# A new issue order for every step of a two-stage kernel (RWKV-7 recurrence, then SwiGLU), with its tiles, operations and bytes kept

## The chip, the cores and the metric

The kernel runs on one NeuronCore of one Trainium2 chip. The metric is device microseconds of one execution, as the median of three runs. Engines are named as the profile does: PE is TensorE's matmuls and PEld its weight loads, DVE is VectorE, ACT is ScalarE, POOL is GpSimd, SP is SyncE. SP and POOL issue nearly all DMAs here, each in the order in which they stand in its own queue.

## What is computed

Everything is float32. The first part is a recurrence over 768 tokens for 4 x 8 heads with a 40 x 40 state; the second part is a gated feed-forward layer over the 3072 tokens of width 320.

```python
for t in range(S):                       # S = 768, per batch and head
    y[:, :, t] = einsum('bhd,bhde->bhe', rt, state)
    Sa = einsum('bhde,bhe->bhd', state, at)
    state = state * wt[:, :, None, :] - einsum('bhd,bhe->bhde', Sa, bt)
    state = state + einsum('bhd,bhe->bhde', vt, kt)
x = y.transpose(0, 2, 1, 3).reshape(3072, 320)
xn = x / sqrt(mean(x * x, -1) + 1e-6) * rms_g
g = xn @ w_gate                          # 320 x 1536
out = (g * sigmoid(g) * (xn @ w_val)) @ w_out
```

## The kernel before

The tokens are worked in 24 chunks of 32, and all 32 heads of a chunk together. Five kinds of stages are written one after another in program text.

- `narrow(k)`, 24 of them: the weights arrive as 64-bit floats, are turned into 32-bit ones with ACT and DVE, and are written back to DRAM as twelve slices `sW0` to `sW11` of 480 KB each.
- `front(c)` for chunk c: loads w and a (tile `wan`), k and b (tile `kbn`), w again (`wn`) and v (`VU`), transposes them on PE, and builds products level by level (matmuls into `ps` from `A`, `Ab` and `K`; results into `KN` and `LT`). It ends by passing a triangular matrix through DRAM (`sB` from `LT`, then `M` from `sB`).
- `inverse(c)`: a chain of 62 dependent DVE operations (`tmp` from `Yi` and `M`, then `Yi` minus `tmp`), through DRAM again (`sY` from `Yi`, `LT` from `sY`). The first four chunks use a shorter form with small matmuls (`M`).
- `main(c)`: the recurrence from chunk to chunk: matmuls from `ST` and `aP` (called state below), from `VU` and `LT` (lower), from `Xs` (lower), from `VU` and `KN` (update), then DVE writes the next `ST`; beside it the scores (`rE`, `vut`), the levels (`As` with `KN` or `kbn`), the output `y`, its norm and its transposition into `xg`.
- `feed(g)` for two chunks together, 12 of them: for each pair of weight slices the loads `wf` from `sW`, matmuls `ps` from `xg` and `wf`, a SiLU on ACT (`sg`), a product on DVE (`hT`), and matmuls `po` from `wf` and `hT`; at the end `o` goes to `out_dram`. Six `wf` buffers hold three pairs, so a load has to wait until the matmuls that read its buffer before are done.

In program text this order isn't issued. Each step becomes a piece of a plan with its engine and its dependences, and `Plan.issue` then issues all 5870 pieces in the order of a table, `ORDER`. A number in it is the distance of the next piece from the first piece that isn't issued yet; a `-` is a filler: one 128 x 128 matmul of the identity into an unused strip of `po` (two matmul records each in the profile, since float32 matmuls take two passes). A second table, `PAIRS`, gives each PSUM result (`room`) one of three bank pairs, `ps0` to `ps2`. Each engine works its own pieces strictly in the issued order, so the tables decide which piece stands ahead of which on each engine and queue; semaphores do the rest.

```python
plan.warm = lambda: nc.tensor.matmul(po_[:, 0, DM:DM + P], ident, ident, start=False, stop=False, skip_group_check=True)
with tc.manual_schedule():
    plan.issue(ORDER, PAIRS)
```

Nearly all instructions of a kind share one line, that of the helper which records them: L503 for DVE, L523, L526 and L529 for ACT, L532 to L538 for POOL, L542 for all DMAs, L545 for matmuls, L548 for transposes, L1077 for the fillers. The profile is therefore read by tiles.

Of the kernel before, what the change touches and what calls it, by code (L numbers as in the profile page):

```python
# [33 lines left out]
- - 4 - 327 - 328 - - - 6 453 5 7 8 9 10 - 11 12 13 14 15 - 16 17 19 18 20 25 26 21 316 325 - - 313 314 324  # L34
323 - 326 318 - 315 317 93 74 83 3 94 85 73 84 82 - 320 46 43 50 61 38 - - - 60 - - 445 444 455 49 58 44 27 56
62 - 333 41 36 48 54 70 - 441 66 53 59 45 638 29 - 32 28 456 55 451 - - - 442 - 334 339 - - 337 335 338 340
349 350 23 - 342 343 354 24 353 22 355 348 351 352 - 344 - 362 336 366 364 95 - 345 367 346 - - - 347 379 360
- - - 361 363 - 359 365 - 375 75 76 376 78 - 79 - 387 77 356 357 - - 373 - 86 378 371 377 - 80 452 446 454 443
57 - 525 636 37 458 34 368 461 - 374 372 89 386 - 369 383 358 462 - 384 370 466 464 465 385 463 478 98 483 495
- 380 467 381 87 468 395 477 - - 470 471 482 - - 481 472 96 492 382 88 494 97 - 99 - 491 476 493 0 328 123 - -  # L40
102 0 - 100 320 - - 121 112 390 389 387 388 102 - - 111 123 392 471 477 487 - 478 486 - 472 98 - - 488 391 79
103 485 473 88 - - - 89 505 626 61 631 69 598 524 633 621 31 67 66 37 395 632 - - 482 - 62 623 622 28 635 625
- 33 396 624 29 397 398 399 483 400 - - 498 401 402 403 404 405 406 407 - - - - - - - 494 499 484 504 - - 394
500 511 502 496 - 104 - 408 409 410 501 411 412 413 414 - 386 - 415 - 503 416 417 418 419 420 421 422 - 641
105 646 - 106 645 643 - 642 - 107 - 423 - 424 425 - 108 497 - 510 - 644 495 426 328 99 330 329 577 427 - - 506
508 509 109 317 319 120 - 90 - 124 647 521 513 - 125 648 113 114 - 115 657 - 522 131 132 576 - 339 507 127 650
651 656 128 - 428 110 142 517 516 - 652 143 518 515 429 - 653 658 512 660 661 - 116 - 654 - 659 117 655 567
860 70 38 - 45 457 65 63 445 446 448 870 861 871 458 447 430 50 - 662 126 568 669 - 133 134 135 578 581 580
579 672 674 - 664 - - - 118 - - - 519 - 520 - - - 431 - - 432 434 433 - 435 - 436 670 437 438 569 572 570 573
571 129 663 673 675 136 137 138 525 683 - 526 527 671 684 467 528 665 529 667 679 668 682 530 531 532 687 680  # L50
686 533 534 535 536 537 538 539 540 685 541 676 677 542 514 543 544 545 546 547 548 549 550 551 552 553 554 -
119 151 140 162 160 - 163 802 141 999 152 666 582 - 574 144 678 681 583 688 147 148 689 555 1000 172 0 761 90
131 535 653 105 516 546 - - 551 - 555 - 564 - 99 659 121 657 658 660 549 550 553 554 552 654 113 650 106 - 114
109 547 655 548 115 116 117 589 590 600 118 0 406 656 590 600 508 548 554 547 825 579 657 700 701 816 509 131
101 643 115 550 551 552 118 642 119 647 702 703 116 117 124 1083 125 126 652 134 653 511 110 512 143 513 510
553 556 557 558 658 559 560 - 120 561 654 831 514 132 826 835 834 515 832 133 135 833 127 128 129 659 660 661
662 663 664 665 666 667 138 142 - 121 516 517 136 137 836 704 706 655 144 708 705 707 - 139 840 - 668 669 670
671 841 - 852 672 848 140 851 853 673 147 674 - 675 148 - 676 865 677 863 861 0 683 - 689 700 694 685 690 684
459 868 693 707 581 708 717 732 734 582 15 579 716 548 712 580 549 713 550 714 719 715 432 585 23 - - 33 21 0
- 394 11 33 32 13 0 26 25 16 861 683 - 417 418 862 681 419 851 749 750 671 571 0 708 701 569 0 569 - 5 6 416  # L60
531 572 689 532 8 533 534 9 708 535 386 704 566 14 15 16 17 - - 0 - 570 569 568 699 529 530 698 567 0 528 700
0 562 713 711 14 698 715 15 559 7 8 712 560 567 710 406 855 16 - 724 427 854 844 21 417 22 568 569 570 571 575
709 716 667 708 - 528 574 573 - 0 23 22 33 520 - 696 782 563 698 784 785 783 697 705 711 567 568 708 709 569
570 571 - 710 398 399 400 401 713 - 847 836 841 830 840 832 842 831 572 769 - - 839 - 829 521 21 0 16 - - 516
712 24 515 710 709 517 711 514 - 841 843 844 842 565 704 840 6 566 848 0 0 0 760 846 856 853 857 564 565 566
712 567 - 569 570 568 - 759 761 842 713 573 - 515 575 574 843 4 852 14 15 16 703 6 844 7 851 17 847 516 5 0
509 568 1243 703 702 846 850 858 0 9 509 858 14 15 16 860 568 569 570 753 523 21 24 23 1241 22 707 708 846 10
709 839 840 710 859 856 754 755 756 757 841 861 711 712 713 850 853 854 714 715 869 716 - 717 718 866 871 872
852 - 855 0 560 561 32 755 513 756 - 857 840 851 854 852 708 862 709 710 711 712 713 714 853 856 - 759 863 864
# [1040 lines left out]
```

## Time and profile before

| What | Value |
|---|---|
| runs, median | 1030.82 us |
| runs, lowest and highest of 3 | 1029.99 and 1036.54 us |
| the profiled execution, its own time | 1040.74 us |
| the profiled execution, its span | 1038.9 us |
| mean granted TensorE clock in it | 0.970 |
| busy in the span: PE, DVE, ACT, POOL | 991.8, 834.2, 452.8, 310.1 us |

The profiled execution took 9.92 us more than the median of the runs and 4.2 us more than the slowest of them, and its span is 1.84 us shorter than its time. Numbers of the trace are those of this one execution; "busy" is time in which an engine had at least one instruction running, and the clock is the share of full speed that PE was granted. "issue" as a releaser means that the engine waited for nothing that the profile shows.

### The profile page before, as it was taken

Reading aid. Unit: us, or ns where it says so; the run is one execution under the profiler, and the core shown is the slowest. Engines: PE = TensorE matmul, PEld = TensorE weight load, DVE = VectorE, ACT = ScalarE, POOL = GpSimd, SP = SyncE. Lnnn points to the kernel's source line nnn. Section 1 sums busy time; section 2 is a strip of 40 time slices with the busy share of each in tenths; the row PEclk is TensorE's granted clock in tenths of the full one; section 3 lists DMA queues with packets and bytes.
Section 4 is the critical chain, followed back from the end, with each engine's and each line's share of the span. In section 5 each row is a group of like instructions: output and inputs, shape, how many; then the busy total and the mean of one; then the engine's idle time right before and its main releaser. Section 6 shows DMA issues by size and latency. Waiting matters only on the chain.

```text
span 1038.9 us, 56159 instructions
## 1 busy us (share of the span) xinstructions
PE 991.8 (95%) x24900; PEld 813.4 (78%) x24900; DVE 834.2 (80%) x2789; ACT 452.8 (44%) x1019; POOL 310.1 (30%) x554
## 2 busy tenths in 40 slices
PE   8968798999999999999999999999999999999998
PEld 7867686888887888888778877878777788787876
DVE  8878777887979898899888798888899789889310
ACT  5755783644452543433533443352334334341210
POOL 9624422231451224142134232242331331210000
PEclk9886898999999999999999999999999999999999
DMA  7676567465443434534433644343524533422322
GB/s 156 155 171 162 156 130 187 127 160 135 124 87 93 120 73 94 131 72 92 127 71 81 139 79 126 94 84 83 140 61 93 136 67 83 130 44 63 87 65 75
DMA packets 163538, 113.03 MB, mean 109 GB/s; under 512 B 124512, under 2 KB 142880, under 8 KB 163296
## 3 DMA queue, kind: packets, MB, share of 16 engines
q1 hardware_dynamic: 144928, 86.48, 32.9%
q0 software_dynamic: 16192, 22.64, 10.9%
q8 instruction: 195, 3.19, 1.3%
q10 hardware_dynamic: 2176, 0.33, 0.3%
q14 instruction: 47, 0.39, 0.1%
HBM read 93.39 MB, written 15.99 MB: 105 GB/s over the span
## 4 chain that ended last, share of the span: by engine, by line
PE 77%; DVE 10%; DMA 4%; issue 4%; ACT 3%; POOL 1%; SPq 1%; ACTq 0%; DVEq 0%; POOLq 0%
PE ps L545 51%; PE po L545 13%; PE ps L548 7%; PE po L1077 5%; DVE LT L503 2%; DVE tmp L503 2%; DVE Yi L503 2%; DVE K L503 1%; DMA kbn<-in_k_dram 1%; SPq L542 1%; DMA wf<-sW 1%; ACT K L526 1%; DVE As L503 1%; ACT KN L526 1%; DMA kbn<-in_b_dram 1%
## 5 line engine op out<-in xcount | busy, mean ns | idle before, releaser
L545 PE MATMUL ps<-xg,wf 128*128 128x256 f32 (+1 forms) x1728 | 356.8, 394 | 1.6 <-DVE ST L503 0.5
L545 PEld LDWEIGHTS ps<-xg,wf 128*128 128x128 f32 (+1 forms) x1728 | 264.7, 191 | 51.1 <-issue 14.0
L545 PE MATMUL po<-wf,hT 128*128 128x320 f32 x576 | 173.6, 440 | 1.7 <-issue 1.1
L523 ACT ACTIVATE sg<-ps 128x512 f32<-128x512 f32 x72 | 43.1, 598 | 231.5 <-PE ps L545 231.4
L503 DVE TENSOR_TENSOR tmp<-Yi,M 128x60 f32<-128x60 f32 (+24 forms) x620 | 131.4, 212 | 15.2 <-DMA M<-sB 1.2
L503 DVE TENSOR_TENSOR Yi<-Yi,tmp 128x60 f32<-128x60 f32 (+24 forms) x620 | 130.8, 211 | 15.0
L545 PEld LDWEIGHTS po<-wf,hT 128*128 128x128 f32 x576 | 103.9, 190 | 37.8 <-issue 2.0
L1077 PE MATMUL po<-ident 128*128 128x128 f32 x580 | 104.0, 315 | 5.9 <-POOL wan L538 3.3
L526 ACT COPY KN<-ps 128x640 f32<-128x640 f32 x96 | 66.5, 693 | 87.4 <-DVE LT L503 57.9
L542 POOL DMA_DIRECT2D kbn<-in_b_dram x92 | 53.6, 585 | 169.7 <-PE ps L545 168.2
L503 DVE TENSOR_TENSOR K<-K,T 128x512 f32<-128x512 f32 (+1 forms) x192 | 93.1, 491 | 4.7 <-ACT K L526 3.2
L1077 PEld LDWEIGHTS po<-ident 128*128 128x128 f32 x580 | 83.1, 210 | 15.5 <-POOL wan L538 3.3
L503 DVE TENSOR_TENSOR hT<-ps,sg 128x512 f32<-128x512 f32 x72 | 49.4, 687 | 53.0 <-ACT sg L523 52.7
L503 DVE TENSOR_TENSOR As<-ps,msi 128x256 f32<-128x256 f32 (+1 forms) x186 | 82.9, 477 | 8.7 <-PE ps L545 7.4
L545 PE MATMUL ps<-Ab,K 40*60 40x56 f32 (+2 forms) x4608 | 78.3, 217 | 11.3 <-issue 6.8
L545 PEld LDWEIGHTS ps<-Ab,K 40*60 40x60 f32 (+2 forms) x4608 | 68.6, 129 | 22.9 <-issue 12.9
L542 POOL DMA_DIRECT2D VU<-in_v_dram x92 | 53.9, 588 | 108.0 <-PE ps L545 57.0
L526 ACT COPY K<-K 128x256 f32<-128x256 f32 (+1 forms) x168 | 73.1, 446 | 29.6 <-DVE K L503 15.1
L542 POOL DMA_DIRECT2D wn<-in_w_dram x92 | 52.2, 569 | 104.7 <-DVE KN L503 81.6
L542 POOL DMA_DIRECT2D kbn<-in_k_dram x92 | 53.7, 586 | 86.0 <-PE ps L545 83.4
L545 PE MATMUL ps<-As,KN 128*40 128x32 f32 x3072 | 71.5, 204 | 8.0 <-issue 8.0
L545 PEld LDWEIGHTS ps<-As,KN 128*40 128x40 f32 x3072 | 64.8, 123 | 16.9 <-issue 13.3
(137 smaller groups left out, 1469.9 us busy)
## 6 DMA issues: line engine op xcount, KB each, us to landing
wf<-sW SPq DMA_DIRECT2D x82, 480.0 KB, 4.7
M<-sB SPq DMA_DIRECT2D x80, 128.0 KB, 3.4
rn<-in_r_dram SPq DMA_DIRECT2D x24, 160.0 KB, 3.9
out_dram<-o SPq DMA_DIRECT2D x48, 80.0 KB, 3.1
kbn<-in_k_dram POOLq DMA_DIRECT2D x92, 40.0 KB, 3.5
kbn<-in_b_dram POOLq DMA_DIRECT2D x92, 40.0 KB, 3.3
wan<-in_w_dram POOLq DMA_DIRECT2D x46, 80.0 KB, 3.0
wan<-in_a_dram POOLq DMA_DIRECT2D x46, 80.0 KB, 3.2
```

The costliest lines, as they stand in the source:

```text
L503: plan.add("DVE", kind, lambda at: fn(at(o), *m(at)), [o], aps(*args))
L523: plan.add("ACT", "act", lambda at: nc.scalar.activation(at(o), at(a), f, **kw), [o] + aps(acc), [a])
L526: plan.add("ACT", "copy", lambda at: nc.scalar.copy(at(o), at(a)), [o], [a])
L542: plan.add(by, "dma", lambda at: queue.dma_start(out=o, in_=i), [o], [i])
L545: return o, lhsT, rhs, lambda at: nc.tensor.matmul(at(o), lhsT, rhs, start=start, stop=stop, skip_group_check=True)
L548: return o, i, ident, lambda at: nc.tensor.transpose(at(o), i, ident)
L1077: plan.warm = lambda: nc.tensor.matmul(po_[:, 0, DM:DM + P], ident, ident, start=False, stop=False, skip_group_check=True)
```

## The change

Only the two tables are replaced. `ORDER` has 6157 entries in place of 6160: the same 5870 pieces, and 287 fillers in place of 290. `PAIRS` keeps its 499 digits, of which many differ, so a PSUM result often lies in another bank pair. The text of `ORDER` is two lines longer, which moves every later line number by two (L545 becomes L547, L548 becomes L550, L1077 becomes L1079). The first lines of both tables, whose numbers tell a reader nothing:

```diff
 ORDER = """
-- - 4 - 327 - 328 - - - 6 453 5 7 8 9 10 - 11 12 13 14 15 - 16 17 19 18 20 25 26 21 316 325 - - 313 314 324
+4 6 5 7 8 49 - 50 70 62 53 9 10 11 12 13 44 - - 65 - 329 - - 63 525 - 453 38 - 43 60 58 - 457 446 397 18 - 14
...
 PAIRS = """
-01210122120010210002012221002102011111200111200020021222201110122022011221100002121101020020012201010121112210
+01201012222220201122102002110011102200011222012212000000012210201201110102122020012022121101111222221100200200
```

What the tables mean is seen in the order of the instructions on each engine. PE's own order changes little: of its 905 pieces 494 keep their rank exactly. Three places, before and after:

First, PE at the start of chunk 3 of the recurrence, some 170 us into the span. `kbn2` and `wan0` here are the inputs of chunk 5, `ST1` and `aP1` feed the state step of chunk 3, `xg0` with `wf` is the first feed. Before:

```order
L548 MATMUL ps0_75<-ident_86,kbn2_111 104x64 x16
L1077 MATMUL po_91<-ident_86 128x128
L548 MATMUL ps1_76<-ident_86,wan0_108 104x64 x16
L545 MATMUL ps2_77<-ST1_117,aP1_147 32x40 x32
L545 MATMUL ps2_77<-VU1_115,LT0_118 32x40 x32
L545 MATMUL ps0_75<-xg0_164,wf0_166 128x256 x2
```

After:

```order
L550 MATMUL ps2_77<-ident_86,wan0_108 104x64 x16
L1079 MATMUL po_91<-ident_86 128x128 x3
L547 MATMUL ps1_76<-ST1_117,aP1_147 32x40 x32
L547 MATMUL ps1_76<-VU1_115,LT0_118 32x40 x32
L550 MATMUL ps2_77<-ident_86,kbn2_111 104x64 x16
L547 MATMUL ps0_75<-xg0_164,wf0_166 128x256 x2
```

The transposes of `kbn2` have moved from ahead of the transposes of `wan0` and of the state and lower matmuls to behind them.

Second, SP's DMA queue some 730 us into the span, in the eighth feed. `wf2` to `wf5` take the slices `sW2`, `sW3`, `sW0`, `sW1` of that feed; `sB`, `M` and `sY` are the passes through DRAM of chunks 18 and 17. Before:

```order
L542 DMA sB0_178<-LT0_118 32x8x32 x4
L542 DMA wf1_167<-sW5_68 128x960
L542 DMA out_0_dram<-o0_176 32x2x320
L542 DMA wf0_166<-sW4_67 128x960
L542 DMA M0_148<-sB0_178 32x1024 x2
L542 DMA out_0_dram<-o0_176 32x2x320
L542 DMA M0_148<-sB0_178 32x1024 x2
L542 DMA sY1_181<-Yi1_151 256x1x32 x3
L542 DMA wf2_168<-sW2_65 128x960
L542 DMA wf3_169<-sW3_66 128x960
L542 DMA sY1_181<-Yi1_151 256x1x32
L542 DMA wf4_170<-sW0_63 128x960
```

After:

```order
L544 DMA sB0_178<-LT0_118 32x8x32
L544 DMA wf2_168<-sW2_65 128x960
L544 DMA sB0_178<-LT0_118 32x8x32 x3
L544 DMA wf1_167<-sW5_68 128x960
L544 DMA wf0_166<-sW4_67 128x960
L544 DMA out_0_dram<-o0_176 32x2x320
L544 DMA wf3_169<-sW3_66 128x960
L544 DMA M0_148<-sB0_178 32x1024 x4
L544 DMA sY1_181<-Yi1_151 256x1x32 x4
L544 DMA wf5_171<-sW1_64 128x960
L544 DMA wf4_170<-sW0_63 128x960
```

The loads of `sW2` and `sW3` have moved 13 and 7 DMAs earlier in the queue, ahead of `sY`; `sW0` and `sW1` stand behind `sY` as before.

Third, SP's queue some 62 us into the span, where the weights are still being converted (`wf` from `in_moe_...` are the raw halves). Before, the load of `wf1` for the first feed:

```order
L542 DMA wf5_171<-in_moe_w_out_dram 128x192
L542 DMA wf5_171<-in_moe_w_val_dram 64x256
L542 DMA wf1_167<-sW1_64 128x960
L542 DMA wf3_169<-in_moe_w_val_dram 128x2x256
L542 DMA rn0_112<-in_r_dram 64x16x40
```

After, the same load:

```order
L544 DMA sW6_69<-o0_176 128x480
L544 DMA wf5_171<-in_moe_w_gate_dram 64x256
L544 DMA wf1_167<-sW1_64 128x960
L544 DMA sY0_180<-M0_148 32x16x16
L544 DMA wf5_171<-in_moe_w_val_dram 64x256
```

It has moved 51 DMAs later, from among the raw loads of slices 3 to 5 to behind the store of `sW6`; its partner `wf0` from `sW0` has moved 27 DMAs earlier.

More of the change, by code (lines that the diff above doesn't have):

```diff
@@ L39 @@
[L39 to L63, printed above, removed]
@@ L259 @@
+00200122222202210020221121022011111121120220010000012000121102111200210222201200222101012000011121120120022201
+02221110111000012012222110020021220012221101111102100002000122211101011120210202121210010200122212010111100100
+12100000101011221122120122201202112211210120220000022110022112121021211022221111020102022000102001111011111121
+20202222020001012102202111022211111102010120001220220120120
 """
```

232 lines of the change are left out of this document (120 added, 112 removed), and 181 rows, old and new, of the table ORDER.

## The prediction

> **What bounds the kernel now.** I read the page first, for who is busy and when.
>
> ```profile
> span 1038.9 us, 56159 instructions
> PE 991.8 (95%) x24900; PEld 813.4 (78%) x24900; DVE 834.2 (80%) x2789; ACT 452.8 (44%) x1019; POOL 310.1 (30%) x554
> PEclk9886898999999999999999999999999999999999
> ```
>
> PE is busy for 95% of the span. No other engine comes near that, and a reordering can't take a matmul away. What it can change is PE's idle time, 1038.9 - 991.8 = 47 us, the fillers, and the time in which PE runs at a lowered clock (the sixes and eights at the left of the clock row). So the next view is PE by stage, first with all of its work and then with the fillers (L1077) alone.
>
> ```profile
> ...
> 40.00:200.00 160.00, 136.46 (x3861) 0.83 0.65 157
> 200.00:960.00 760.00, 745.44 (x19434) 1.00 0.42 100
> 960.00:1039.00 79.00, 74.53 (x901) 1.00 0.25 75
> ```
>
> ```profile
> ...
> 40.00:200.00 160.00, 38.31 (x197) 0.83 0.65 157
> 200.00:960.00 760.00, 40.16 (x200) 1.00 0.42 100
> 960.00:1039.00 79.00, 0.00 (x0) 1.00 0.25 75
> ```
>
> The columns are the stretch, its length, PE's busy time, the granted clock, the DMA engines' busy share and GB/s. From 200 to 960 us PE is idle for 14.6 us of 760 and fills another 40.2 us with fillers; the tail has no filler and 4.5 us idle. Between 40 and 200 us it is idle for 23.5 us, and at a clock of 0.83 it gives up 0.17 x 160 = 27 us of full speed. So the early stretch is where most can be won or lost; from 200 us on, PE's own matmuls set the pace.
>
> What PE waits for is in the view of waits:
>
> ```profile
> PE ps L545 <- issue: 24.9, 21, 4.2
> PE ps L548 <- DMA kbn<-in_k_dram: 0.9, 1, 0.9
> PE po L1077 <- ACT o L526: 1.9, 2, 1.0
> ```
>
> Most of it, 24.9 us in 21 waits, has no releaser: PE stops in the middle of a group of matmuls whose operands are there. Two of these, with the 5-us windows around each:
>
> ```profile
> 65.43 0.94 PE L545 MATMUL ps<-Ab,K 40*56 40x56 f32 x54
> 70.57 0.53 PE L545 MATMUL ps<-Ab,K 40*56 40x56 f32 x10 [4.20 <-issue]
> ...
> 741.40 0.56 PE L545 MATMUL ps<-A,K 40*64 40x56 f32 x22 [1.96 <-issue]
> ```
>
> ```profile
> 65.00:70.00 5.00, 1.36 (x64) 0.98 1.17 213
> 70.00:75.00 5.00, 4.43 (x96) 0.50 1.06 250
> 75.00:80.00 5.00, 3.23 (x136) 0.50 0.29 86
> 80.00:85.00 5.00, 5.00 (x103) 0.66 0.46 97
> ...
> 90.00:95.00 5.00, 4.40 (x113) 0.52 0.95 220
> 95.00:100.00 5.00, 2.69 (x127) 0.50 0.95 259
> 100.00:105.00 5.00, 5.00 (x115) 0.61 0.37 107
> ...
> 170.00:175.00 5.00, 4.14 (x78) 0.72 1.09 229
> 175.00:180.00 5.00, 4.81 (x147) 0.50 0.49 127
> 180.00:185.00 5.00, 5.00 (x28) 0.76 0.48 141
> ...
> 725.00:730.00 5.00, 5.00 (x102) 1.00 0.99 265
> 735.00:740.00 5.00, 4.43 (x150) 1.00 0.98 317
> 740.00:745.00 5.00, 3.60 (x30) 0.72 0.21 40
> ...
> 815.00:820.00 5.00, 3.42 (x113) 1.00 0.93 239
> 820.00:825.00 5.00, 4.74 (x71) 0.66 0.20 46
> ```
>
> Each stop stands in a window in which the DMA engines are busy for 0.9 or more, and a lowered clock follows it. Not each busy window has a stop: 725 to 730 us, at 0.99, has none. My reading is that PE's instructions come through the same engines:
>
> ```profile
> q8 instruction: 195, 3.19, 1.3%
> ```
>
> These are 195 packets of 3.19 MB / 195 = 16.4 KB. [...]
>
> **The change, part by part.** All sums are against the profiled execution, 1040.74 us; what is worked out for it is then carried to the median of 1030.82.
>
> 1. Fillers: 287 for 290, so six records fewer, at 40.16 / 200 = 0.20 us each by the row above: 1.2 us. If PE merely idles in their place, nothing. Ends -1.2 and 0; I take the middle, -0.6.
>
> 2. The transposes of `kbn2` at 171 us, moved behind `wan0`, state and lower. What they wait for:
>
> ```profile
> 165.75 6.74 DMA kbn<-in_k_dram
> ...
> 172.62 1.07 PE L548 MATMUL ps<-ident,kbn 64*104 64x64 f32 x15 [0.86 <-DMA kbn<-in_k_dram]
> ...
> 170.63 0.82 DVE L503 TENSOR_TENSOR ST<-ps,Sdec 128x640 f32<-128x640 f32 x1
> ...
> 175.37 0.50 PE L545 MATMUL ps<-ST,aP 40*32 40x40 f32 x26
> ```
>
> The first row is from the chain of work that ended last, the others from the timeline. The last k load lands at 172.5 us, and PE waits 0.86 us for it. `ST` is written by 171.45, yet state starts at 175.37, as it stands behind `kbn2` and `wan0`. In the new order state can run while the load is under way, and the transposes come after it; the wait goes, and ahead of the recurrence one group of transposes (1.07 us) is gone. Late next are chunk 5's first products; they stand behind the feed's matmuls (`ps` from `xg0` and `wf`) in both orders, and those cover them. The clock drop behind this place costs (0.28 + 0.50 + 0.24) x 5 = 5.1 us of full speed by the rows for 170 to 185; whether it goes too isn't shown, as another stop lies ahead of it. Ends -6.0 and 0. I take the wait alone, -0.9, the row that is nearest.
>
> 3. The burst at 725 to 740 us. In SP's queue four `wf` loads of 480 KB stood between 731 and 736 us; two now stand ahead of `sY` and can go when their buffers are free.
>
> ```profile
> 731.25 1.82 SPq L542 DMA_DIRECT2D wf<-sW  x2
> 733.12 0.56 SPq L542 DMA_DIRECT2D sY<-Yi  x1
> 734.80 1.40 SPq L542 DMA_DIRECT2D wf<-sW  x2
> ...
> SPq L542 <- PE po L545: 228.3, 48, 30.6
> ```
>
> The stop there is 1.96 us and the clock after it loses 0.28 x 5 = 1.4 us: 3.4 us in all. Against it stands the last row: SP waits 228.3 us in 48 waits for `po` matmuls to free a buffer, and a load that is put earlier holds up the queue behind it, here three `sB` transfers and `M`, on which chunk 18's inverse waits. DVE has a chain of another chunk to work meanwhile, so I price that at nought, with 3.4 us as its upper end (one more stop of this kind). Half of the loads leave the burst; I take half of the stop, -1.7.
>
> 4. The early loads. `wf1` from `sW1` (480 KB) leaves the burst at 62 to 75 us, whose stop of 4.20 us and clock loss of (0.50 + 0.50 + 0.34) x 5 = 6.7 us make 10.9 us. It moves 51 places down the queue, to some 91 us by the times of SP's rows, where the windows 90 to 100 already show 0.95 of the DMA engines and up to 259 GB/s. What is won at the one place can be paid at the other. Ends -10.9 and +10.9; the bytes are the same and both bursts are full, so I take 0.
>
> 5. The burst at 815 us. One `wf` load of the ninth feed goes five places down SP's queue, nearer to that burst. Its stop is worth 5 - 3.42 = 1.6 us and the clock 0.34 x 5 = 1.7: ends 0 and +3.3. It lands in the stretch before it, in which the page shows no stop; I take 0.
>
> 6. The other moves: 2542 of DVE's 2786 pieces and 411 of PE's 905 change rank, mostly by less than 2 us of the engine's own work, and other `ps` pairs are used. PE's queue is full from 200 us on (745.44 of 760), which covers these. If the cover is gone, one wait is about a microsecond (1.9 us in 2 waits for `o`, above), or 3.4 us where it ends in a lowered clock. I take 0.
>
> Sum: -0.6 - 0.9 - 1.7 = -3.2 us, which makes the profiled execution 1037.5. The timed runs have fewer stops to lose: the profiled one is 9.9 us above their median, and if that is of the same kind as its 24.9 us of stops and 27 us of clock, the runs keep (51.9 - 9.9) / 51.9 = 0.8 of it. So 0.6 + 0.8 x 2.6 = 2.7 us come off 1030.82: **1028 us**.
>
> [...]
>
> **The rivals.**
>
> - Slower: the early burst only moves. With `wf1` among the loads at 90 to 100 us, PE gets one more stop like that at 66 us there: 10.9 us, and 0.6 to 3.4 us for a further one in the middle, without the gains of terms 2 and 3. That gives 1030.8 + 10.9 + 0.6 = 1042 us, up to 1045. For it: the 0.95 windows, and that two stops in 90 to 105 us already cost (0.48 + 0.50 + 0.39) x 5 = 6.9 us of clock. Against it: 95% of PE's work has a stable queue, and the raw loads around it have shifted as well. It decides from one whole stop with its lowered clock upward.
> - Faster: the early burst is really broken up. 10.9 us from term 4 at 65 us, and 3.4 us from term 3: 1030.8 - 14.3 = 1016.5. For it: 27 us of lost clock lie in 160 us. Against it: 157 GB/s over that whole stretch must still be moved, and 38 us of fillers in it are time in which PE waits for other engines.
> - Nothing of it matters: PE's order is nearly the same and the stops fall elsewhere by chance; 1030.8, within the middle case. [...]
>
> **How the numbers follow.** A difference of 1% (10.3 us, 1020.5 to 1041.1) is about what a measurement of this kernel can tell from no change. The forecast with "nothing matters" holds 0.66; the slower rival 0.22; the faster rival 0.12. All of the middle case lies within 1%, so the chances are 0.12, 0.66 and 0.22. The range takes in the forecast, most of the slower rival to its upper end, 1045, and the faster one to within 1.5 us of its value, 1018; a tenth or less is left out on each side.
>
> **What would show it.** Right: no wait for `kbn` at 172 us and state starting before its transposes; a DMA share below 0.9 at 735 to 740 us with a clock of 1.00 behind it; PE busy over 745 us of 760 again. Wrong: a clock under 0.83 over 40 to 200 us, or more than 21 stops on "issue"; more DVE waiting for `M` or `LT` loads after 700 us, which would say that SP's queue was held up by an early `wf` load. The forecast is wrong altogether if PE's idle time from 200 to 960 us changes by more than 10 us, since I hold that stretch to be covered.

## The result and the profile after

The changed kernel takes 1070.85 us (median of 4 runs, 1060.06 to 1082.89) where the kernel before takes 1033.68 us beside it (4 runs, 1029.99 to 1039.42). The ratio is 1.0324 with a 95% interval of 1.0263 to 1.0385: it is slower by 3.2%. The profiled execution, 1082.89 us, fell into a slower state than the other three (1060.06 to 1074.22 us) and is left out of the ratio. Forecast were 1028 us and no difference that can be measured. All ratios below are against runs of the kernel before on the same chip; its own median lay between 1033.7 and 1041.2 us on the chips used.

The trace of the profiled execution is the only one of the change, so I use it for where the time goes and the other runs for how much it is. First its page, as for the kernel before:

```profile
span 1081.0 us, 56071 instructions
PE 1011.6 (94%) x24894; PEld 827.9 (77%) x24894; DVE 836.5 (77%) x2789; ACT 448.5 (41%) x1019; POOL 310.4 (29%) x554
PEclk9976888999999999999999899999899999999999
```

Then the mean clock of the execution, before and after:

```profile
core 0: 1038.9 us, clock 0.970
```

```profile
core 0: 1081.0 us, clock 0.953
```

The span has grown by 42.1 us, and two parts make nearly all of it. PE is idle for 1081.0 - 1011.6 = 69.4 us where it was 47.1: 22.3 us more. And at a clock of 0.953 it gives up 0.047 x 1081.0 = 50.8 us of full speed where it was 0.030 x 1038.9 = 31.2: 19.6 us more. PE's matmuls are the same; the change made stops, and in this execution the clock behind the stops costs about as much again. By the trace's clock records there are 16 spells at half clock in place of 8, 104.3 us in place of 63.3. In the other three executions the clock was 0.965 to 0.968 over spans of 1058.1 to 1072.2 us, which gives up 34 to 38 us; seven executions of the kernel before, on another chip, gave up 18 to 34, on average 27. So there the clock takes some 9 us of a loss of 33, by my estimate a quarter and not a half; in a_mid and a_sp below it takes 15 to 17 of 31 to 35.

PE by stage (length, busy time, clock, share of the DMA engines, GB/s) and its largest waits (us in total, times, longest):

```profile
0.00:40.00 40.00, 32.10 (x571) 0.96 0.79 159
40.00:200.00 160.00, 133.88 (x3698) 0.80 0.59 144
200.00:960.00 760.00, 731.68 (x18878) 0.98 0.43 99
960.00:1081.00 121.00, 113.94 (x1786) 0.99 0.25 71
```

```profile
PE ps L547 <- issue: 14.6, 12, 3.2
PE ps L550 <- issue: 5.7, 4, 2.1
PE ps L547 <- DMA M<-sY: 5.3, 4, 2.4
PE ps L550 <- DVE y L505: 4.4, 4, 2.9
PE ps L547 <- ACT Xs L531: 3.5, 1, 3.5
```

From 200 to 960 us PE is idle for 28.3 us, not 14.6, and the clock is 0.98, not 1.00. The stops on "issue" have not become more: 14.6 us against 24.9, and with all lines together 21.6 against 26.7. What is new are PE's waits for the other engines and for transfers, spread over many rows of some microseconds: 16.5 us for DVE, 14.1 for ACT and 10.8 for transfers, where it was 6.3, 4.2 and 1.9. To see where they arise I took, for the same piece of PE's work, its start in the trace after less its start before (the lag):

| place, by the trace before | lag gained | PE idle, before and after | clock lost, before and after |
|---|---|---|---|
| 0 to 40 us | 9.1 us | 4.6, 7.7 us | 0.0, 3.4 us |
| 130 to 170 us | 7.0 us | 2.9, 6.0 us | 2.3, 6.8 us |
| 225 to 285 us | 4.8 us | 0.0, 2.3 us | 0.0, 1.7 us |
| 570 to 600 us | 11.6 us | 0.0, 4.5 us | 0.0, 5.1 us |
| 860 to 1000 us | 10.1 us | 1.7, 7.6 us | 0.0, 3.4 us |
| all the rest | -1.2 us | | |

So it is not one place, and not an even spread either: five places in which PE runs dry for 2 to 6 us, with the clock down behind most of them. The sizes are those of one execution of each kernel, and executions differ: s_tail, d_dve, d_act, b_extra, b_qtr and t_mid below issue the same first 1500 entries as the kernel before, and at 225 us they lie 4 to 13 us ahead of its trace. So the first two rows say where PE stops, but not how much is lost there. In the traces of a_mid and a_sp below, which keep the order of the computing engines of the change, the same pieces have stops of the same size: ahead of and within the second gram product (`Ab` with `K`) of chunk 0 2.43, 2.03 and 1.64 us, ahead of the second one of chunk 1 2.03, 1.99 and 2.03, ahead of and within the scores of chunk 2 1.99, 1.48 and 1.90.

### The profile page after: what moved, and what is told of

Its sections match the earlier page's. It is cut to its first block, busy times and chain, and to the rows that moved or that the text cites. A ratio compares the mean times of both kernels' runs of the same rounds, so it can differ in the third digit from the quotient of the medians.

```text
span 1081.0 us, 56071 instructions
## 1 busy us (share of the span) xinstructions
PE 1011.6 (94%) x24894; PEld 827.9 (77%) x24894; DVE 836.5 (77%) x2789; ACT 448.5 (41%) x1019; POOL 310.4 (29%) x554
## 3 DMA queue, kind: packets, MB, share of 16 engines
q0 software_dynamic: 16192, 22.64, 10.9%
q8 instruction: 195, 3.19, 1.3%
## 4 chain that ended last, share of the span: by engine, by line
PE 63%; DVE 16%; DMA 9%; SPq 4%; issue 4%; ACT 3%; ACTq 0%; POOL 0%; DVEq 0%
PE ps L547 43%; PE po L547 12%; PE ps L550 5%; SPq L544 4%; PE po L1079 4%; DVE tmp L505 2%; DVE Yi L505 2%; DVE LT L505 2%; DMA wf<-sW 2%; DMA M<-sB 2%; DVE K L505 1%; DVE y L505 1%; DVE Ab L505 1%; DMA LT<-sY 1%; DMA wf<-in_moe_w_out_dram 1%
## 5 line engine op out<-in xcount | busy, mean ns | idle before, releaser
L547 PE MATMUL ps<-xg,wf 128*128 128x256 f32 (+1 forms) x1728 | 362.4, 399 | 5.6 <-issue 2.7
L547 PEld LDWEIGHTS ps<-xg,wf 128*128 128x128 f32 (+1 forms) x1728 | 269.2, 194 | 57.0 <-issue 15.4
L547 PE MATMUL po<-wf,hT 128*128 128x320 f32 x576 | 180.0, 450 | 0.8 <-ACT o L528 0.8
L505 DVE TENSOR_TENSOR Yi<-Yi,tmp 128x60 f32<-128x60 f32 (+24 forms) x620 | 130.4, 210 | 14.5
L547 PEld LDWEIGHTS po<-wf,hT 128*128 128x128 f32 x576 | 106.2, 194 | 37.9 <-issue 3.4
L1079 PE MATMUL po<-ident 128*128 128x128 f32 x574 | 104.1, 319 | 5.9 <-DVE po L579 3.3
L505 DVE TENSOR_TENSOR K<-K,T 128x512 f32<-128x512 f32 (+1 forms) x192 | 93.2, 491 | 10.9 <-ACT K L528 8.5
L1079 PEld LDWEIGHTS po<-ident 128*128 128x128 f32 x574 | 84.8, 215 | 14.5 <-POOL M L537 3.3
L547 PE MATMUL ps<-Ab,K 40*60 40x56 f32 (+2 forms) x4608 | 81.1, 221 | 13.5 <-issue 4.8
L505 DVE TENSOR_TENSOR As<-ps,msi 128x256 f32<-128x256 f32 (+1 forms) x186 | 81.7, 476 | 15.5 <-PE ps L547 12.4
L547 PEld LDWEIGHTS ps<-Ab,K 40*60 40x60 f32 (+2 forms) x4608 | 71.4, 132 | 25.5 <-issue 12.3
L547 PEld LDWEIGHTS ps<-As,KN 128*40 128x40 f32 x3072 | 65.1, 125 | 10.0 <-issue 5.6
L547 PE MATMUL ps<-As,KN 128*40 128x32 f32 x3072 | 70.9, 205 | 0.1
```

Source lines behind the costliest of these rows:

```text
L505: plan.add("DVE", kind, lambda at: fn(at(o), *m(at)), [o], aps(*args))
L547: return o, lhsT, rhs, lambda at: nc.tensor.matmul(at(o), lhsT, rhs, start=start, stop=stop, skip_group_check=True)
```

## The experiments

Three theories stood at the start. Theory 1: SP's queue. It works in order (below, a `wf` load whose buffer is free at 586.7 us goes at 599.43, behind an `M<-sB` that waits until 599.06), and in the new order urgent transfers stand behind transfers that wait. Theory 2: the order of the computing engines is itself the longer one. Theory 3: the old order fits the chip to fractions of a microsecond, and any other loses. A fourth came up on the way: transfers take longer than the new order leaves room for.

### Halves of the change: q_after, q_before, s_head, s_tail

Each takes a part of the new table. "Q" stands for the queues of SP and POOL, "C" for PE with its fillers, DVE, ACT and `PAIRS`. The dependences don't allow either mixture in full: 10 of SP's and 30 of POOL's instructions in q_after, 8 and 19 in q_before, stand at another place than in the queue that was meant.

```diff
 ORDER, PAIRS:
-C before, Q before
+q_after:  C before, Q of the change
+q_before: C of the change, Q before
+s_head:   first 1500 entries (to about 219 us) of the change, the rest before
+s_tail:   first 1500 entries before, the rest of the change
```

> The order of before on PE, DVE and ACT (fillers and bank pairs too), with SP's and POOL's queues in the order of the change. Theory Q (the DMA queues' order costs the time: a DMA placed early waits at the head of SP's queue and holds up what is needed behind it): 25 to 35 us over before. Theory C (the order on PE, DVE and ACT, or the bank pairs, cost it): within 8 us of before.

> The reverse: PE, DVE and ACT, fillers and pairs of the change, with SP's and POOL's queues in the order of before. Theory Q: within 8 us of before. Theory C: 25 to 35 us over before. If both hybrids are slow by about half, or both by the whole, the two orders belong together and neither alone is the cause.

> The first 1500 entries of the changed table (some 225 us, the stage in which the weights are still converted), then all that remains in the order of before. The two traces part by 16 us up to there and by 26 us after it. If the loss is laid down where the traces part: 12 to 18 us over before. If the later steps are caused by the state that the early stage leaves behind: 25 to 35 us.

> The first 1500 entries of before, then the rest in the changed order. If the loss is laid down where the traces part: 15 to 26 us over before. If the early stage causes the later steps: within 8 us of before.

Measured, all four on one chip: q_after 1124.09 us, ratio 1.0815 [1.0743, 1.0888]; q_before 1110.19 us, 1.0685 [1.0626, 1.0745]; s_head 1057.11 us, 1.0162 [1.0103, 1.0222]; s_tail 1058.33 us, 1.0158 [1.0084, 1.0231]. In time the two parts cost the same, and 1.0162 x 1.0158 = 1.0323 is the whole, within intervals of some 0.7%. Between engines it can't be cut at all: either mixture is over twice as bad as the change. That fits two orders that are made for each other; neither can be called the bad one from these two runs.

### SP's queue: a_mid, a_sp, b_sp, and random order: j_small

At 570 to 600 us the trace after shows a queue that is held up. SP's issues there, and the matmul that waits:

```profile
590.08 0.30 SPq L544 DMA_DIRECT2D sB<-LT  x1
...
593.91 0.56 SPq L544 DMA_DIRECT2D sY<-Yi  x1
599.06 0.32 SPq L544 DMA_DIRECT2D M<-sB  x1
599.43 0.42 SPq L544 DMA_DIRECT2D wf<-sW  x1
```

```profile
606.69 1.19 PE L547 MATMUL ps<-xg,wf 64*128 64x256 f32 x4 [1.87 <-DMA wf<-sW]
```

`M<-sB` has to wait until the stores `sB` have landed, and SP does nothing from 594.5 to 599.06. Behind it stand a `wf` load, whose buffer has been free since 586.7 us, and three of the four stores `sY`, whose data are there since 593.85. PE runs out of weights at 604.82. a_mid mends this place alone, a_sp sorts the whole queue by when data are there and when they are needed, b_sp does the same to the kernel before, and j_small shakes the order of before.

```diff
 SP's queue at this place, the change (-) and a_mid (+):
-sB<-LT, wf<-sW, sB<-LT x2, wf<-sW, sB<-LT, sY<-Yi, M<-sB, wf<-sW, M<-sB, sY<-Yi, M<-sB x2, sY<-Yi x2
+wf<-sW x3, sB<-LT x4, sY<-Yi x3, M<-sB x4, sY<-Yi
 a_sp, b_sp: 502 and 429 of SP's 634 transfers at another place; all else as it was
 j_small: before, neighbours in the table swapped at random, 20 tries for each entry (one such order; PAIRS as before)
```

> The change with 23 of SP's transfers at one place (those issued between 583 and 611 us of its trace) in another order: the loads of rounded weights for chunk 5 of the expert part and the stores sY<-Yi of inverse 13 no longer stand behind the store sB<-LT of front 14 and the loads M<-sB after it. PE, DVE, ACT and POOL keep the change's order. Theory 1 (SP's queue: an urgent transfer stands behind one that waits, PE runs dry for 2 to 4 us, and the clock is halved behind the gap): the lag of the change behind the kernel before, which grew by 11.6 us between 570 and 600 us of before, grows there by under 4; the time is about 8 us below the change's 1070.9, near 1063. Theory 2 (the order of the computing engines itself is the longer one there): 1071, no difference of over 3 us, and main 13 starts as late as in the change.

> The change with SP's whole queue sorted anew: each transfer goes when its data are there, by the trace of the change, and among those that are there the one whose user starts first; 502 of 634 stand at another place. All other engines keep the change's order. Theory 1 (SP's queue holds what the change lost): 15 to 30 us are given back, 1040 to 1055, and DVE's, ACT's and PE's waits for transfers fall from 67 us together to under 35. Theory 2 (the computing engines' order): 1065 to 1075, with the waits for transfers turned into waits for engines. Theory 3 (any order but the one that was measured and kept loses a few per cent): over 1071.

> The control for the run before: the same sorting of SP's queue, by the trace of before, laid on the kernel before; 429 of 634 transfers stand at another place. Theory 1: before has next to no waits for transfers (1.4 us on DVE, 1.9 on PE), so there is nothing to give back: 1028 to 1040. Theory 3 (any other order loses): 1050 or more, since transfers at another place mean other bursts.

> The kernel before, its order shaken at random: neighbours in the table change places again and again (20 tries for each entry, where data and PSUM allow it), so that PE has 424 pairs of pieces in the other order (the change has 444), DVE 2769 (11876), ACT 755 (2270), SP 876 (2248). No piece moves far: at most 13 places on DVE, 11 on SP. Theory 3 (the old order fits the chip to fractions of a microsecond, and any change of it loses): 3% or more, 1065 to 1100. Theories 1 and 2 (a few places of the change where something waits): moves that short meet few waits, 1030 to 1050.

Measured, on one chip: a_mid 1068.85 us, ratio 1.0276 [1.0197, 1.0355]; a_sp 1072.24 us, 1.0310 [1.0232, 1.0388]; b_sp 1053.96 us, 1.0133 [1.0052, 1.0213]; j_small 1464.77 us, 1.4128 [1.3980, 1.4276]. SP in a_mid at this place:

```profile
579.17 5.09 SPq L543 DMA_DIRECT2D wf<-sW  x3
585.65 1.81 SPq L543 DMA_DIRECT2D sB<-LT  x4
589.48 1.87 SPq L543 DMA_DIRECT2D sY<-Yi  x3
```

Locally theory 1 holds: the lag gained there falls from 11.6 to 3.9 us, the wait for `wf` is gone, and no half clock follows (1.00 from 585 to 620 us). In the time a_mid is 0.5% nearer to before, which its interval can't tell from nothing. As the theory of the whole loss it falls with a_sp: DVE's and ACT's waits for transfers drop from 56 us together to 23 by the trace, just as wanted, and the time stays, as theories 2 and 3 had forecast. PE's own waits for transfers did not drop, 14.5 us for 10.8; the largest of them has grown from 5.3 us:

```profile
PE ps L542 <- DMA M<-sY: 12.5, 5, 5.3
```

b_sp shows that the same sorting makes the kernel before slower by 1.3%, against theory 1, which expected 1028 to 1040, and in line with theory 3, which expected 1050 or more. And j_small is the largest surprise of the study. No piece moved over 13 places on DVE or 11 on SP, PE has fewer pairs in another order than in the change, and 41% are lost:

```profile
span 1458.5 us, 56074 instructions
...
PE 1171.1 (80%) x24900; PEld 924.4 (63%) x24900; DVE 829.5 (57%) x2789; ACT 450.7 (31%) x1019; POOL 309.8 (21%) x554
```

PE is idle for 287 us, and its busy time has grown by 179 us, with a clock of 0.839 in place of 0.970. By its waits it stands 147.5 us for DVE, 88.9 for ACT and 27.6 for transfers, and only 17.4 on "issue". Theory 3 said 3% or more, so its direction holds; its size, 1065 to 1100 us, does not. Next to this the change's order is a good one: 3.2% lost with four times as many pairs moved on DVE. How many pieces move thus doesn't tell the loss by itself.

### Short delays and cheaper transfers: d_dve, d_act, b_extra, b_qtr, a_qtr

The first two ask how much cover there is in the kernel before, that is, how late other engines may be while PE still has work in its queue; b_extra is their control. The other two load a quarter of the columns of `wf` for chunks 2 to 11 of the feed, so part of the weights is left out.

```diff
 d_dve, d_act (b_extra: the tile and its memset alone)
-        for word in order.split():
+        for n, word in enumerate(order.split()):
+            if n in range(1500, 5700, 70):
+                self.late()
+    slow = const.tile([P, 120], FP32, name="slow")
+    nc.gpsimd.memset(slow, 0.0)
+    plan.late = lambda: [nc.vector.memset(slow, 0.0) for _ in range(3)]                     # d_dve
+    plan.late = lambda: [nc.scalar.copy(slow[:, 60:120], slow[:, 0:60]) for _ in range(2)]  # d_act
 b_qtr (on before), a_qtr (on the change)
-                    dma(wf, sW[f + e])
+                    w = WF if g < 2 else WF // 4
+                    dma(wf[:, 0:w], sW[f + e][:, 0:w])
```

> The kernel before with 60 extra stops of DVE, one at every 70th entry of the table from entry 1500 to 5700 (about 215 to 960 us): each three memsets of 128x120 on a tile that nothing reads, 0.3 to 0.6 us of DVE (a 128x60 operation takes 0.21 us), 18 to 36 us in all. Nothing else changes. If the prediction's cover holds (PE has its queue full there, so that work of other engines may come half a microsecond later at no cost): 1034 to 1038. If there is no such cover (each piece of DVE is handed over just in time): a third to all of the added DVE work shows as time, plus the clock that is halved behind the new gaps: 1050 to 1080.

> The same with ACT: 60 stops of two copies of 60 columns within a tile that nothing reads, 0.3 to 0.6 us of ACT each. ACT is busy for 41 to 43% of the span, DVE for 80%. If the cover holds: 1034 to 1038. If ACT's pieces are handed over just in time though the engine is idle for more than half of the time: 1045 to 1070.

> The kernel before with one more tile of 128x120 and the one memset of it on POOL that the two kernels with added stops had, without the stops: a control for them, since ACT's stops came out 9 us faster than before. If the stops themselves help (later copies, so PE runs less often into a gap): the time of before, a ratio of 0.998 to 1.002. If the tile or the memset (other addresses, POOL a fifth of a microsecond later) make the gain: a ratio of 0.988 to 0.995.

> The kernel before, with the loads of rounded weights for chunks 2 to 11 of the expert part cut to a quarter of their columns (480 KB become 120); the columns left out keep the weights of an earlier slice, so this leaves out part of the input of those chunks. Every instruction and wait stays. Before hardly waits for transfers (3 us in all): 1025 to 1036 by every theory.

> The same cut in the change's kernel (part of the weights of chunks 2 to 11 isn't loaded). The change lies 37 us behind before, about 20 of them after 285 us, where the cut works. If late transfers carry the loss (the order leaves less room for the time that they take on the chip): the 20 us after 285 us shrink to under 8, so that this kernel is at 1048 to 1060, 15 to 25 us above the one before with the same cut. If the loss lies in the order of the computing engines: 1064 to 1075, 30 us or more above it.

Measured: d_dve 1044.90 us, ratio 1.0068 [1.0028, 1.0109]; d_act 1030.22 us, 0.9925 [0.9879, 0.9971]; b_qtr 1028.28 us, 0.9915 [0.9868, 0.9961]; a_qtr 1058.39 us, 1.0184 [1.0109, 1.0259], these four on one chip; b_extra, on another, 1031.52 us, 0.9984 [0.9948, 1.0021]. What was added, busy time and mean duration:

```profile
L576 DVE MEMSET slow<- 128x120 f32 x180 | 28.4, 158 | 11.1
```

```profile
L576 ACT COPY slow<-slow 128x60 f32<-128x60 f32 x120 | 29.0, 242 | 1.9
```

28.4 us of DVE work in stops of 0.47 us cost 0.7%, some 7 us (3 to 11), a quarter of it, when the kernel before is the measure. Beside d_act, on the same chip and with the same extra tile, it is 1044.90 - 1030.22 = 14.7 us, a half; and by the trace d_dve leads before by 13.4 us at 225 us, where its stops begin, and by nothing at the end. So a quarter to a half. 29.0 us of ACT work cost nothing. So the cover that the prediction counted on does exist for delays of half a microsecond, on ACT in full, on DVE in part. d_act is even 0.8% below before, but I don't put that down to its stops: by the trace its lead of 9.9 us is there at 225 us, ahead of nearly all of them, and stays at 8.7 to 10.5 us from there on. b_extra, without stops, leads by 8.0 us there too, so that it is rather the trace of before that is late. In the runs b_extra shows no gain, though the two intervals touch; what makes the 0.8% stays open.

The pair with cheaper loads is 1058.39 - 1028.28 = 30.1 us apart, where the whole kernels are 37.2; by the ratios it is 1.0184 / 0.9915 = 1.027 for 1.032, less apart than the intervals are wide. In the profiled executions the change gains 21 us of lag behind 285 us; with the cut it gains 1.7 on before, and 11 on before with the cut, which itself wins 9.4 us there. So by the traces, one execution each, transfers carry a part of the second half, perhaps a half of it; the times don't settle it. Of the first half this pair says nothing, as nothing was cut there. The total is at the bound that was written down for theory 2. What b_qtr won shows in these windows; it runs some 4 us ahead there, and in the second fence, its place of the stop at 818 us, 8 to 12:

```profile
725.00:730.00 5.00, 5.00 (x112) 1.00 0.56 111
730.00:735.00 5.00, 5.00 (x136) 1.00 0.49 98
735.00:740.00 5.00, 5.00 (x116) 1.00 0.02 5
```

```profile
805.00:810.00 5.00, 5.00 (x172) 1.00 0.77 158
810.00:815.00 5.00, 5.00 (x110) 1.00 0.38 74
```

With the DMA engines at 0.77 or less PE has no stop in either place and a clock of 1.00. Both stops of the kernel before, 1.96 and 1.84 us on "issue", came with the burst of weight loads and went with it.

### The first 45 us: w_start, w_start_c, w_start_q, b_raw

Here every trace with the change's order has a lag, and those with the old order have none (9.1, 5.7 and 7.0 us at 40 us in the change, a_mid and a_sp; -0.5 to +1.5 in s_tail, b_sp, d_dve, d_act and b_qtr, which keep the old order there).

```diff
 the first 431 entries of ORDER (front 0 and 1, the first raw weights), all else before:
+w_start:   the change's order (with 4 fillers more and 8 other digits of PAIRS)
+w_start_c: the change's order of DVE and ACT only (158 and 70 instructions at another place)
+w_start_q: the change's order of SP and POOL only (73 and 90)
 b_raw, SP's queue, all else before:
-sB<-LT x4, wf<-in_moe_w_gate x2, ..., wf<-in_moe_w_val, ..., wf<-in_moe_w_out
+wf<-in_moe_w_gate x2, wf<-in_moe_w_out, wf<-in_moe_w_val, sB<-LT x4, ...
```

> The kernel before with the first 431 entries of the table (about 45 us: the raw loads, front 0 and 1) in the change's order. At 40 us of before the change lies 6 to 9 us behind; kernels that keep the old order there lie within 0.5 us of it. If this place is a loss of its own: 5 to 9 us behind at 40 us, the same or less at the end, 1037 to 1046. If the lag is made up later (PE stands idle there anyway, and the fillers only fill): under 3 us at 285 us.

> Only DVE and ACT in the change's order among those 431 entries (158 and 70 instructions at another place), PE with its fillers, SP and POOL as before. If the order of the computing engines makes the lag (ACT has a copy KN<-ps, which waits for PE's gram product of front 0, ahead of the copy K<-K that PE's next gram product needs): 4 us or more behind at 40 us. If the queues or the fillers make it: under 2 us.

> Only SP and POOL in the change's order among those 431 entries (73 and 90 at another place), the rest as before. If the order of the transfers makes the lag: 4 us or more behind at 40 us. If the order of the computing engines does: under 2 us.

> The kernel before with four transfers moved in SP's queue and nothing else: the raw weight loads wf<-in_moe_w_gate_dram of narrow 3 and 4, wf<-in_moe_w_out_dram of narrow 5 and a wf<-in_moe_w_val_dram of narrow 3 go ahead of the four stores sB<-LT of front 0 (at about 16 us) and not 4 to 18 places behind them, as in the change. If the fuller burst of transfers makes the lag that all three kernels with the change's queue order have at 20 us: the DMA share over 16 to 22 us goes from 0.74 and 0.55 to about 1.1, PE stops for 1.5 to 2.5 us within its gram products with nothing that it waits for, the clock is halved for some us behind it, and the kernel lies 2 to 4 us behind at 20 us; the time is 1 to 6 us above before. If another of the 73 moves in SP's queue or the 90 in POOL's makes it: no stop over 0.5 us, under 1 us behind at 20 us.

Measured: w_start 1054.17 us, ratio 1.0133 [1.0070, 1.0195]; w_start_c 1059.32 us, 1.0147 [1.0068, 1.0227]; w_start_q 1050.11 us, 1.0105 [1.0037, 1.0173]; b_raw 1041.78 us, 1.0023 [0.9988, 1.0059]. So 431 entries of 6157 make 1.3% by themselves. Both halves alone make the lag, 16.2 and 7.2 us at 40 us, where together they make 5.8; so these runs don't say which of them it is. What each does can be read, though. PE (length, busy, clock, DMA share, GB/s) before, then in w_start_q, with the stop in it:

```profile
16.00:19.00 3.00, 3.00 (x80) 1.00 0.74 205
19.00:22.00 3.00, 2.56 (x94) 1.00 0.55 123
22.00:25.00 3.00, 2.41 (x66) 1.00 0.26 57
```

```profile
16.00:19.00 3.00, 2.97 (x60) 1.00 1.19 180
19.00:22.00 3.00, 0.57 (x26) 0.99 1.09 172
22.00:25.00 3.00, 3.00 (x38) 0.50 0.85 158
```

```profile
18.20 0.77 PE L546 MATMUL ps<-Ab,K 40*60 40x56 f32 x39
...
21.43 0.56 PE L546 MATMUL ps<-Ab,K 40*60 40x56 f32 x25 [2.46 <-issue]
```

The new queue order puts more raw weight loads ahead of the first `sB`. The DMA engines are full to 22 us, PE stops in the middle of a gram product that has all its operands, and its clock halves. In w_start_c it is ACT's order: ACT stands for 11.67 us at a conversion, for raw weights whose load the old queue issues at some 39.5 us and the queue of the change at 14. Behind it stands a copy that PE's second gram product of chunk 1 needs, and PE stands for 10.71 us. Here one can see an order of ACT that needs its own order of the queue:

```profile
42.24 0.72 ACT L524 ACTIVATE xg<-wf,ctop 128x480 f32<-128x480 int16 x1 [11.67 <-DMA wf<-in_moe_w_out_dram]
...
47.44 1.86 PE L546 MATMUL ps<-Ab,K 40*60 40x56 f32 x64 [10.71 <-ACT KN L527]
```

b_raw moved just four of these loads. The burst came (0.82, 1.03 and 0.83 in the three windows), and a stop came too, but of another kind than expected: 3.65 us for a late `wan` load, with half clock behind it.

```profile
25.24 0.26 PE L549 MATMUL ps<-ident,wan 64*104 64x64 f32 x1 [3.65 <-DMA wan<-in_a_dram]
```

The lag, 8.4 us at 40 us, melts to 1.8 at 225 (against a trace of before that is itself late there, as said above), and in the time nothing is left that can be measured. So the early loads make a stop, but not the one on "issue" of w_start_q: from 19 to 22 us the DMA engines were at 1.03, nearly as in w_start_q, and PE's gram product ran through. Which of the other moves makes that one stays open. A stop in the first 60 us needn't show in the time; in w_start it did.

### Do the places of the second half add up? t_mid

```diff
 ORDER, PAIRS:
-entries 1500 to the end of the change (s_tail)
+entries 1500 to 5440 (219 to 856 us) of the change, SP mended as in a_mid, then before
```

> The change's order only for entries 1500 to 5440 of the table (about 219 to 856 us), with the 23 transfers of 583 to 611 us mended as in a_mid; the rest in before's order. The kernel with the old first 1500 entries and the change behind them was 1.6% slower, and its trace lost 9 us at 570 to 600 us, 9 at 860 to 1000 and about 6 in small steps at 225 to 470. If the loss sits at places and these two are most of it: 0.0 to 0.8% above before. If it is made anew wherever the old and the new order meet, or moves to other places when one is mended: 1.2% or more.

Measured: 1055.09 us, ratio 1.0115 [1.0065, 1.0165], against 1.0158 for s_tail: the two mended places return 0.4% where 1.6% was to be explained, which the intervals can't tell from nothing. The result lies between the two forecasts, at most 0.8% and 1.2% or more, and nearer to the second. Its trace gains 9.2 us of lag between 285 and 470 us, where the same order gained 1.1 in the change and 5.9 in s_tail, and a new stop stands some 20 us behind the point where the old order takes over:

```profile
890.64 0.27 PE L546 MATMUL ps<-r,Sd 40*40 40x32 f32 x2 [2.88 <-issue]
```

So mending two places did not take their part out of the time, and stops stand at others. How the loss divides between the five places thus stays open.

## Why the prediction was wrong, step by step

- **Step 6 failed**, the other moves at nought because "PE's queue is full from 200 us on (745.44 of 760), which covers these". The sign that it named for this came: PE's idle time from 200 to 960 us went from 14.6 to 28.3 us, by more than 10. What the runs put in its place: cover there is, but for half a microsecond (d_act lost none, d_dve a quarter to a half of the added work), not for what the table moves. PE's waits for DVE, ACT and transfers went from 12.4 to 41.4 us. I had written "mostly by less than 2 us", which holds for 1660 of the 2542 pieces of DVE that move; by the times of the trace before the other 882 move by more than 2 us of their engine's time and 81 by more than 10, and on SP 110 of 634 by more than 10. That it is these far moves which cost is argued; no run moves them alone. A busy share is a mean: of 791 PE pieces after 200 us that take something from another engine or a load, 226 start within 2 us of it by my reckoning from the trace before (a load counted as landed 3 us behind its issue, where the medians of the loads in that trace are 2.6 to 4.8 us), and those have no cover for such moves. j_small shows that short moves, at most 13 places on DVE, can cost far more when nothing arranges them, 41%.
- **The price of a stop, also step 6.** It put one lost cover at "about a microsecond" or 3.4 us and counted none. By the profiled execution it was some ten of 1 to 4 us and nearly as much again by the clock, 22.3 + 19.6 us; in the other executions the clock takes less, as said above.
- **Step 1, fillers, -0.6.** Nothing came off: from 200 to 960 us PE runs 206 filler records for 200, and 40.55 us for 40.16. It was the end at nought.
- **Step 2, the transposes of `kbn2`, -0.9.** The order does what was said: state starts ahead of the transposes and nothing waits for `kbn` there. But two stops on "issue" take the place of the wait, 1.34 us each for 0.86, so the place loses 1.8 us and gains nothing:

```profile
185.93 0.56 PE L547 MATMUL ps<-ST,aP 40*32 40x40 f32 x39
187.83 0.35 PE L547 MATMUL ps<-ST,aP 40*32 40x40 f32 x25 [1.34 <-issue]
188.11 0.79 PE L547 MATMUL ps<-VU,LT 32*32 32x40 f32 x64
190.24 1.19 PE L550 MATMUL ps<-ident,kbn 64*104 64x64 f32 x16 [1.34 <-issue]
```

- **Step 3, the burst at 725 to 740 us, -1.7.** That the stop comes with the burst of loads was right: b_qtr, with a quarter of the bytes, has none. That earlier places would thin the burst was wrong: 30 us later by the clock, after, the DMA engines are at 1.01 from 755 to 760 us, and then:

```profile
760.00:765.00 5.00, 5.00 (x132) 1.00 1.06 265
765.00:770.00 5.00, 2.87 (x59) 0.72 0.83 164
770.00:775.00 5.00, 5.00 (x55) 0.50 0.18 41
775.00:780.00 5.00, 5.00 (x80) 0.76 0.50 164
```

  The share below 0.9 that was named as a sign is there, at 765 us, and means nothing: the burst ends with the stop, 2.13 us by its row in the timeline. The clock loses (0.28 + 0.50 + 0.24) x 5 = 5.1 us behind it. In sum 7.2 us for 3.4, so +3.8 and not -1.7, beyond the upper end of +3.4.
- **Step 4, the early loads, 0 within 10.9.** Between 40 and 200 us PE is idle for 26.1 us, not 23.5, and the clock of 0.80 costs 0.03 x 160 = 4.8 us more: about +7, inside the bounds, but not by the balance that the step had in mind. Without the load of `wf1` the burst at 65 to 75 us is still there, at 1.01 and 0.91 of the DMA engines (1.17 and 1.06 before), and PE stops in it for 3.53 us on ACT's `Xs` and 3.19 us on "issue" with 23.89 us of half clock behind, where it was 4.20 us and 13.65. The clock under 0.83 was named as a sign of the slower rival. That rival had its price from a new stop at 90 to 100 us; in the trace of the change 9 us were lost before 40 us already, which no step and no rival looked at.
- **Step 5, the burst at 815 us, 0.** The stop of 1.84 us is gone, in its place PE waits 0.84 us for DVE's `y` and 1.12 us for ACT's `x`, at full clock: 2.0 us for 3.3, outside the bounds on the good side, and too small to matter.
- **The signs.** "More DVE waiting for `M` or `LT` loads after 700 us", which was to say that SP's queue is held up by an early `wf` load, came, though it is small; the trace before has no such wait there:

```profile
DVE tmp L505 <- DMA M<-sB: 5.1, 3, 3.4
```

  "More than 21 stops on issue" did not come; the row has 12. The forecast sought the danger in stops on "issue", since those were most of PE's waits before (26.7 of 42.4 us); the change brought waits for DVE, ACT and transfers, which the trace before hardly shows. That each stop on "issue" stands in a window at 0.9 or more was also misread: in the prediction's own fence 75 to 80 us has one of 1.77 us at 0.29. Nor has each a lowered clock behind it: those of 1.05, 0.83 and 1.09 us ahead of 519.67, 643.48 and 887.41 us have a clock of 1.00 in the 5 us that hold them and in the 10 us behind. The slower rival had the direction, but with one more early stop as its cause and 1045 us as its end.

What is shown: the loss is PE's stops and the clock behind them; it arises in the first and in the second part of the table alike; it does not come from SP's order alone, nor from short delays on ACT, nor, by the one pair of traces, from the bytes of the weight loads alone. What is open: how it divides between the order of the computing engines and that of the queues, which the mixtures tried here could not separate without making new stops. The bank pairs were not tried by themselves: 326 of the 499 digits differ, and they always went with "C"; b_sp and j_small lose with the pairs of before, so new pairs aren't needed for a loss, but what they add here isn't known.

## What to carry to other kernels

When the whole order of a tuned kernel is replaced, don't add up the two or three moves that can be named and take the rest as nought: the rest is the change, and the trace before, in which PE hardly waits for other engines or transfers, can't show what it will wait for. Look instead at how many pieces of the bound engine start just after their input, and at what stands ahead of urgent transfers in queues that work in order, as SP's did here from 594.5 to 599.06 us (that such a count foretells the loss was not tried here). Price a stop of PE at itself and the half clock that can follow it: here 22.3 us more of idle time came with 19.6 us more of lost clock in the profiled execution, and in the others the clock takes some 9 us of 33 by my estimate.

## What the hardware did that I had not expected

- By the clock records of the traces before and after, the spells at half clock last 3.41, 6.83, 10.24, 13.65 or 23.89 us: one to four and seven times 3.41 (but for the last one of a trace, which its end cuts). A stop of 1.33 us at 97 us of the change was followed by a spell of 10.24 us; that costs 5.1 us of full speed, nearly four times the stop.

```profile
96.91 0.71 PE L1079 MATMUL po<-ident 128*128 128x128 f32 x4 [1.33 <-issue]
```

- PE's stops on "issue" often come with the load on the DMA engines: with the same order on PE one appears at 19 us when the share goes from 0.55 to 1.09 (w_start_q), and two vanish at 739 and 818 us when it drops to 0.77 or less (b_qtr). But load is not needed: in the change PE stops for 1.85 us in a gram product at 910 us, where the DMA engines stand still but for one packet, and that one is of the instruction queue. What the stops do share is a packet of the instruction queue (q8) ahead of their end: all 20 of over 0.3 us in the trace before end 1.3 to 2.1 us after such a packet, of 16,384 bytes, has landed, and 16 of the 17 in the trace after 1.2 to 2.1 us. That agrees with the prediction's reading that PE's instructions come through the same engines. That a burst makes the packet late isn't shown: in the trace before the 20 packets took 0.92 to 2.18 us, with a median of 1.09, and all 195 have a median of 1.06; the other 175 pass without such a stop. The stop, and the window around it (length, busy, clock, DMA share, GB/s):

```profile
911.56 0.74 PE L547 MATMUL ps<-Ab,K 40*48 40x56 f32 x41 [1.85 <-issue]
```

```profile
905.00:912.00 7.00, 5.14 (x196) 1.00 0.01 2
```

- 29.0 us of added work on ACT in 60 short stops cost nothing, and one random exchange of close neighbours 41%. From 215 us on the kernel bears it when ACT is late by a little; other orders cost it from nothing that can be measured (b_raw, four transfers) to 41%.
